# First 512 tokens of a retention layer with its feed-forward block: k and v loaded four tokens to a partition, the work by head pairs on 32-row groups

## The chip, the core and the metric

The kernel runs on one core of one Trainium2 chip. A core has TensorE (PE, matmuls; PEld are its weight loads), VectorE (DVE), ScalarE (ACT), GpSimd (POOL) and SyncE (SP), which here only issues DMAs. Each engine works through its own instruction queue in order and waits on semaphores for the others. The metric is the device time of one execution in microseconds (us).

## The reference

A retention (a recurrent attention with decay) over 4 batches, 8 heads, 768 tokens and head width 64, followed by a feed-forward block over all 3072 tokens.

```python
gamma = 1.0 - 2.0 ** (-5.0 - np.arange(H))
for t in range(S):
    state = gamma[None, :, None, None] * state + np.einsum('bhd,bhe->bhde', k[:, :, t], v[:, :, t])
    y[:, :, t] = scale * np.einsum('bhd,bhde->bhe', q[:, :, t], state)
x = y.transpose(0, 2, 1, 3).reshape(B * S, H * D)
h = x @ w_in                       # 512 -> 2048
g = h * np.tanh(softplus(h))       # Mish
out = g @ w_out                    # 2048 -> 512
```

## The kernel before

Tokens are taken in chunks of C = 128; 24 chunks in all, six to a batch. Retention is done chunkwise: the powers of gamma are folded into q and v when they are cast to 16 bit, k is only scaled. For a chunk, "scores" multiplies k and q (per head, contraction over 64), "mask" keeps the causal part on VectorE (`am`), "present" multiplies v and `am`, "past" multiplies the state and q, and both add up in `y_ps`. "outer" makes k times v, which with the state before and the decay of a chunk (`gcm`) gives the next `state`. Heads are handled in pairs: one head on partitions 0 to 63, the other on 64 to 127, HP = 4 pairs. `xt` takes y for the feed-forward matmuls.

The feed-forward block works on blocks of tokens: first one of 512 tokens (TB; CPB = 4 chunks), then blocks of 256. For the first block `g1` (L412) makes `h_ps`, 16 groups of four matmuls with 512 columns, each followed by a Mish on ScalarE (L420); `g2_mm` (L426) then makes `o_ps`. The matmuls of later blocks carry the retention of the chunks ahead in between, at places that `plan` and `plan_of` write out by hand. The order of instructions on each engine is that of the program (`manual_schedule`); the framework adds the waits.

`first_block` (L570) is the part that has nothing to hide behind. It loads q for all 512 tokens with four neighbouring tokens in one partition (`load_first_q`, L177: runs of 1 KB in memory, two DMAs of 512 KB), k and v chunk by chunk (`load_one`, L120: one token to a partition, runs of 256 B, 256 KB each), and then the weights (`load_weights`, L550: w_in in slices, w_out after it). All these loads are issued by SP, in this order. Since q's tokens stand by residue (token 4p + r), its transpose `qfirst_t` is kept as [pair, r, p], and the scores of chunk g read columns 32g to 32g + 31 of each r; the mask `tri_first` has its columns in the same order, and so has y until `xt_first` (L336) puts it in `xt`. The output of the block is stored in the same order (L434).

The loop at L589 takes the four chunks one after the other: scores, mask (L283), y of the chunk before, outer product with the state before added by an identity matmul (L296), turning k of the next chunk (L206, copied at L208), new state (L303). The last chunk's y is done in two halves. `spin` (L243) and `spin_quarters` (L251) are filler matmuls on the identity, whose results are overwritten. k is scaled on ScalarE (L220), v on POOL (L223). Then `cast_win` (L152) casts w_in on VectorE, half a slice at a time, and the `g1` groups start.

PSUM has two pools: `mmps` (tag "mm", four buffers: t_ps, u_ps, y_ps, h_ps, o_ps) and `atps` (tag "at", two buffers of double size).

## Time and profile before

| what | us |
|---|---|
| runs of the kernel, median of 3 (lowest, highest) | 208.75 (208.70, 208.92) |
| span of the profiled execution, first to last instruction | 206.5 |
| first cast of q starts | 5.26 |
| first chunk's scores (L273) start | 9.84 |
| last cast of v starts | 17.29 |
| last two casts to xt start (L358) | 18.73 |
| h_ps starts (L412) | 19.49 |
| o_ps starts (L426) | 33.55 |

The profile is of one execution; its own device time beside the span isn't recorded, the span is 2.25 us below the median of the runs. In the page, busy times are sums over the span; the chain of waits follows the last instruction back to what released it; the timeline gives start and duration of merged instructions; the windows give busy time per engine in a stretch. The granted clock of TensorE is 0.999 over the span.

### The profile page before, as it was taken

Reading aid. Unit: us, or ns where it says so; the run is one execution under the profiler, and the core shown is the slowest. Engines: PE = TensorE matmul, PEld = TensorE weight load, DVE = VectorE, ACT = ScalarE, POOL = GpSimd, SP = SyncE. Lnnn points to the kernel's source line nnn. Section 1 sums busy time; section 2 is a strip of 40 time slices with the busy share of each in tenths; the row PEclk is TensorE's granted clock in tenths of the full one; section 3 lists DMA queues with packets and bytes.
Section 4 is the critical chain, followed back from the end, with each engine's and each line's share of the span. In section 5 each row is a group of like instructions: output and inputs, shape, how many; then the busy total and the mean of one; then the engine's idle time right before and its main releaser. Section 6 shows DMA issues by size and latency. Waiting matters only on the chain.

```text
span 206.5 us, 4747 instructions
## 1 busy us (share of the span) xinstructions
PE 200.1 (97%) x2005; PEld 151.0 (73%) x2005; DVE 120.7 (58%) x184; ACT 86.5 (42%) x146; POOL 76.2 (37%) x72
## 2 busy tenths in 40 slices
PE   7899999999999999999999999999999999999993
PEld 2465444455855865788888888888888888898882
DVE  2697454267019998475585774495675773572062
ACT  2243664142631541453453453453453453552640
POOL 3242000427866555578665265156266000000000
PEclk9999999999999999999999999999999999999999
DMA  5999999999899999999999798499894800200202
GB/s 175 237 219 345 381 387 355 233 296 208 176 205 292 195 228 207 213 238 253 209 218 152 168 195 149 115 246 154 200 241 71 206 0 2 105 0 27 77 25 76
DMA packets 99988, 38.59 MB, mean 187 GB/s; under 512 B 90496, under 2 KB 94080, under 8 KB 99968
## 3 DMA queue, kind: packets, MB, share of 16 engines
q1 hardware_dynamic: 96704, 37.50, 82.4%
q10 hardware_dynamic: 3264, 0.81, 2.4%
q8 instruction: 15, 0.25, 0.5%
q14 instruction: 5, 0.04, 0.1%
HBM read 27.29 MB, written 6.29 MB: 163 GB/s over the span
## 4 chain that ended last, share of the span: by engine, by line
PE 83%; SPq 7%; DMA 5%; DVE 1%; ACT 1%; issue 1%; ACTq 0%
PE h_ps L412 38%; PE o_ps L506 23%; PE o_ps L426 13%; SPq L122 5%; DMA wi<-in_moe_w_in_dram 5%; PE y_ps L323 3%; PE at L273 3%; PE y_ps L313 2%; SPq L140 2%; PE u_ps L291 2%; ACT xt L400 1%; DVE gsum L476 1%; SPq L181 0%; DVE win L157 0%; PE t_ps L261 0%
## 5 line engine op out<-in xcount | busy, mean ns | idle before, releaser
L412 PE MATMUL h_ps<-xt,win 128*128 128x256 f16 (+1 forms) x704 | 88.0, 282 | 0.4 <-ACT xt L400 0.2
L420 ACT ACTIVATE g<-h_ps 128x512 f16<-128x512 f32 x96 | 57.3, 597 | 57.6 <-PE h_ps L412 57.6
L412 PEld LDWEIGHTS <-win 128*128 128x128 f16 x704 | 67.9, 98 | 16.9 <-DVE win L157 0.9
L217 POOL TENSOR_TENSOR qk<-qf,qvs 128x512 f16<-128x512 f32 x20 | 21.5, 1077 | 61.6 <-DMA qf<-in_q_dram 52.3
L283 DVE TENSOR_TENSOR am<-at,tri 128x1024 f16<-128x1024 f32 x20 | 23.7, 1220 | 17.1 <-PE at L273 16.9
L223 POOL TENSOR_TENSOR v<-vf,qvs 128x512 f16<-128x512 f32 x24 | 25.4, 1059 | 18.6 <-DMA vf<-in_v_dram 17.0
L426 PE MATMUL o_ps<-wout,g 128*128 128x512 f16 x128 | 30.1, 380 | 0.0
L222 POOL TENSOR_SCALAR qk<-kf 128x512 f16<-128x512 f32 x18 | 27.7, 1540 | 2.0 <-DMA kf<-in_k_dram 0.7
L506 PEld LDWEIGHTS <-gsum 128*128 128x128 f16 x256 | 24.4, 98 | 3.8 <-DVE gsum L476 0.4
L506 PE MATMUL o_ps<-tmat,gsum 128*128 128x256 f16 x192 | 23.7, 273 | 0.1
L426 PEld LDWEIGHTS <-g 128*128 128x128 f16 x128 | 11.7, 98 | 13.0 <-issue 0.3
L520 DVE TENSOR_TENSOR osb<-o_ps,snap 128x256 f32<-128x256 f32 x24 | 10.1, 422 | 18.8 <-ACT snap L512 15.7
L506 PEld LDWEIGHTS <-g 128*128 128x128 f16 x192 | 18.8, 98 | 2.2
L400 ACT CAST xt<-y_ps 128x1024 f16<-128x1024 f32 x10 | 10.1, 1012 | 21.7 <-PE y_ps L323 21.7
L475 DVE TENSOR_TENSOR gsum<-g 128x512 f16<-128x512 f16 x16 | 7.6, 472 | 13.6 <-ACT g L420 13.6
L506 PE MATMUL o_ps<-wout,g 128*128 128x256 f16 x128 | 15.3, 273 | 0.0
L512 ACT COPY snap<-o_ps 128x256 f32<-128x256 f32 x24 | 8.9, 372 | 14.0 <-PE o_ps L506 14.0
L306 DVE TENSOR_TENSOR su<-u_ps,st 128x512 f32<-128x512 f32 x13 | 9.0, 691 | 4.7 <-PE u_ps L291 4.5
L307 DVE TENSOR_TENSOR st<-su,gcm 128x512 f16<-128x512 f32 x13 | 9.8, 754 | 0.4
L243 PE MATMUL at<-ident 128*128 128x512 f16 (+1 forms) x26 | 8.0, 440 | 1.3 <-POOL ident L81 1.3
L220 ACT ACTIVATE qk<-kf 128x512 f16<-128x512 f32 x6 | 3.8, 630 | 12.4 <-DMA kf<-in_k_dram 12.4
L157 DVE CAST win<-wi 128x1024 f16<-128x1024 f32 x8 | 5.4, 692 | 5.3 <-DMA wi<-in_moe_w_in_dram 5.3
(61 smaller groups left out, 150.0 us busy)
## 6 DMA issues: line engine op xcount, KB each, us to landing
kf<-in_k_dram SPq DMA_DIRECT2D x23, 256.0 KB, 4.9
vf<-in_v_dram SPq DMA_DIRECT2D x23, 256.0 KB, 5.0
out_dram<-osb SPq DMA_DIRECT2D x22, 256.0 KB, 4.0
qf<-in_q_dram SPq DMA_DIRECT2D x19, 256.0 KB, 4.4
wt<-in_moe_w_out_dram SPq DMA_DIRECT2D x3, 1024.0 KB, 10.1
wi<-in_moe_w_in_dram SPq DMA_DIRECT2D x4, 512.0 KB, 6.9
wi<-in_moe_w_in_dram SPq DMA_DIRECT2D x2, 1024.0 KB, 10.3
qfirst<-in_q_dram SPq DMA_DIRECT2D x2, 512.0 KB, 5.0
```

What stands on the lines that cost most here:

```text
L122: queue.dma_start(loaded[g][n], (q, k, v)[n][b, :, c * C:(c + 1) * C].rearrange("h p d -> p h d"))
L217: nc.gpsimd.tensor_tensor(q16, qf, qs.unsqueeze(2).broadcast_to((P, H, D)), op=ALU.mult)
L222: nc.gpsimd.tensor_scalar(k16, kf, BOOST, None, op0=ALU.mult)
L223: nc.gpsimd.tensor_tensor(v16, vf, vs.unsqueeze(2).broadcast_to((P, H, D)), op=ALU.mult)
L283: nc.vector.tensor_tensor(am[:, :, i:i + n], at[:, :, i:i + n], keep.unsqueeze(1).unsqueeze(1).broadcast_to((P, 2, n, C)), op=ALU.mult)
L307: nc.vector.tensor_tensor(st, su, gcm, op=ALU.mult)
L400: nc.scalar.copy(xt[:, :, :2 * C], y_ps.rearrange("p i j c -> p i (j c)"))
L412: nc.tensor.matmul(h_ps[:, j], wins[s][f // 2][:, bp, f % 2 * P:(f % 2 + 1) * P], xts[blk][:, bp, :nt], start=(bp == 0), stop=(bp == NBP - 1))
L420: nc.scalar.activation(gt, h_ps, AF.Mish, scale=inv_boost3)
L426: nc.tensor.matmul(o_ps, gts[blk, fb][:, t * P:(t + 1) * P], wouts[s][:, f, cols], start=(fb == 0), stop=(fb == NFB - 1))
L506: nc.tensor.matmul(o_ps, x(f), w(f), start=first and f == 0, stop=f == n - 1, skip_group_check=True)
L520: nc.vector.tensor_tensor(dst, o_ps, plus, op=ALU.add)
```

## The change

For the first 512 tokens k and v are loaded like q, four tokens to a partition, and all three by head pairs: twelve DMAs of 256 KB with runs of 1 KB, in the order q0 k0 q1 k1 v0 v1 q2 k2 v2 q3 k3 v3 (`first_loads`). A partition now holds tokens of one chunk in each group of 32 rows (chunk c on rows 32c to 32c + 31). So the work goes by pairs, not by chunks: a pair's scores for all four chunks are 32 matmuls, whose weights are 64 rows by 32 columns (`score_pair`); outer products and "present" take weights of 32 rows by 64 columns; neighbouring matmuls lie on other rows. One mask per pair covers the four chunks; `tri_first` is now made of four selects on POOL and four copies on VectorE. States inside the block are kept as [128, pair, 64] in `early`, and stepped through the chunks by `state_steps`; the state after the fourth chunk goes to the old form. For pair 3 the states are stepped on ScalarE. The first two groups of h_ps are cut into halves: the part over pairs 0 and 1 ahead of the last y, the other part after it (`g1_part`); the half slice of w_in for it is cast on POOL. Of the filler matmuls 28 and 4 (in units of 128 columns) are left. The rest of the program is the same.

```diff
...
-    spread = [qs_np[(jj * CPB + r) % C] for r in range(CPB)]
-    qvs_np = np.ascontiguousarray(np.concatenate([qs_np, vs_np, *spread], 1))
+    spread = [(jj * CPB + r) % C for r in range(CPB)]
+    qvs_np = np.ascontiguousarray(np.concatenate(
+        [qs_np, vs_np] + [qs_np[j] for j in spread] + [vs_np[j] for j in spread], 1))
...
-    tpp = ctx.enter_context(tc.tile_pool(name="rn_tp", bufs=2))
+    tpp = ctx.enter_context(tc.tile_pool(name="rn_tp", bufs=4))
...
+    late = cpool.tile([P, 2 * CPB - 1, Q0], FP32, name="late")
+    tri_first = cpool.tile([P, CPB, CPB, Q0], FP32, name="tri_first")
+    nc.gpsimd.memset(late, 0.0)
+    for c in range(CPB):
+        t = late[c * Q0:(c + 1) * Q0]
+        nc.gpsimd.affine_select(
+            out=t, in_=t, compare_op=ALU.is_gt, fill=1.0, base=CPB - 1,
+            pattern=[[-1, 2 * CPB - 1], [-CPB, Q0]], channel_multiplier=CPB)
...
+    for h in range(H):
+        o = 64 * (h % 2)
+        nc.vector.memset(gc[o:o + 64, h // 2], float(gamma[h] ** C))
+    for r in range(CPB):
+        nc.vector.tensor_copy(tri_first[:, r], late[:, CPB - 1 - r:2 * CPB - 1 - r])
...
-    def cast_win(s):
...
+    def cast_win(s, half, eng):
...
-    def load_first_q():
-    def turn_first_q(qf, half, on_act):
-    def turn_k(g):
-    def spin_quarters(g, n, width):
-    def outer_one(g):
-    def xt_first(g, pairs=slice(None)):
-    def y_one(g):
-    def y_one_in_halves(g):
...
+    def g1_part(h_ps, u, part):
+        for bp in range(2 * part, 2 * part + 2):
+            nc.tensor.matmul(
+                h_ps[:, 0], win(0, u, bp), xts[0][:, bp], start=(bp == 0), stop=(bp == NBP - 1),
+                skip_group_check=True)
...
+    def first_loads():
+        for nm, i in (("q", 0), ("k", 0), ("q", 1), ("k", 1), ("v", 0), ("v", 1),
+                      ("q", 2), ("k", 2), ("v", 2), ("q", 3), ("k", 3), ("v", 3)):
+            t = lpool.tile([P, 2, CPB, D], FP32, name=nm + "f", tag=nm + "f", bufs=4 if nm == "q" else 6)
+            nc.sync.dma_start(
+                t, dict(q=q, k=k, v=v)[nm][0, 2 * i:2 * i + 2, :TB].rearrange(
+                    "h (p r) d -> p h r d", r=CPB))
+            raw[nm, i] = t
+        nload[0] = ncast[0] = CPB
+        load_weights()
...
+    def cast_pair(nm, i, eng):
+        if nm == "q":
+            qk16[i] = castp.tile([P, 2, CPB, 2, D], FP16, name="qk16")
+        if nm == "v":
+            v16p[i] = castp.tile([P, CPB, 2, D], FP16, name="v16")
+        dst = (v16p[i] if nm == "v" else qk16[i][:, "qk".index(nm)]).rearrange(
+            "p r h d -> p h r d")
+        src = raw.pop((nm, i))
+        if nm == "k":
+            nc.scalar.mul(dst, src, BOOST)
+        else:
+            by = (qs_spread if nm == "q" else vs_spread)[:, 2 * i:2 * i + 2]
+            eng.tensor_tensor(
+                dst, src, by.unsqueeze(3).broadcast_to((P, 2, CPB, D)), op=ALU.mult)
+
+    def turn_pair(nm, i, eng):
+        n = "qk".index(nm)
+        if i not in turned:
+            turned[i] = (mmps.tile([P, 2, CPB, P], FP16, name="t_ps", tag="mm"),
+                         qktp.tile([P, 2, CPB, P], FP16, name="qkt", bufs=4))
+        t_ps, qkt = turned[i]
+        for r in range(CPB):
+            nc.tensor.transpose(t_ps[:, n, r], qk16[i][:, n, r], ident)
+        if eng is nc.scalar:
+            nc.scalar.copy(qkt[:, n], t_ps[:, n])
+        else:
+            eng.tensor_copy(qkt[:, n], t_ps[:, n])
+        qkt2[i] = qkt
+
+    def score_pair(i, at):
+        for r in range(CPB):
+            for c in range(CPB):
+                for hh in range(2):
+                    o = slice(64 * hh, 64 * hh + 64)
+                    nc.tensor.matmul(
+                        at[rows(c), hh, r], qkt2[i][o, 1, r, rows(c)],
+                        qkt2[i][o, 0, :, rows(c)], start=True, stop=True,
+                        skip_group_check=True)
+
+    def mask_pair(i, at, hh=slice(0, 2)):
+        if i not in amp:
+            amp[i] = tpp.tile([P, 2, CPB, C], FP16, name="am")
+        nc.vector.tensor_tensor(
+            amp[i][:, hh].rearrange("p a r t -> p a (r t)"),
+            at[:, hh].rearrange("p a r t -> p a (r t)"),
+            tri_first.rearrange("p r a t -> p (r a t)").unsqueeze(1).broadcast_to(
+                (P, hh.stop - hh.start, CPB * C)), op=ALU.mult)
+
+    def state_steps(pairs, on_act=False):
+        n = len(pairs)
+        u_ps = [mmps.tile([P, 2, n, D], FP32, name="u_ps", tag="mm") for _ in range(2)]
+        for c in range(CPB):
+            if c % 2 == 0:
+                for j, i in enumerate(pairs):
+                    for r in range(CPB):
+                        for cc in (c, c + 1):
+                            for hh in range(2):
+                                nc.tensor.matmul(
+                                    u_ps[cc % 2][64 * hh:64 * hh + 64, cc // 2, j],
+                                    qk16[i][rows(cc), 1, r, hh], v16p[i][rows(cc), r, hh],
+                                    start=c == 0 and j == 0 and r == 0, stop=r == CPB - 1,
+                                    skip_group_check=True)
+            u = u_ps[c % 2][:, c // 2]
+            here = slice(pairs[0], pairs[-1] + 1)
+            if c > 0:
+                nc.tensor.matmul(
+                    u, ident, early[c - 1][:, here], start=False, stop=True,
+                    skip_group_check=True)
+            if c == CPB - 1:
+                for hh in range(2):
+                    o = slice(64 * hh, 64 * hh + 64)
+                    nc.vector.tensor_tensor(
+                        states[c][o, here, o], u[o], gc[o, here], op=ALU.mult)
+            elif on_act:
+                for j, i in enumerate(pairs):
+                    nc.scalar.mul(early[c][:, i], u[:, j], gc[:, i, :1])
+            else:
+                nc.vector.tensor_tensor(early[c][:, here], u, gc[:, here], op=ALU.mult)
+            yield
+
+    def y_at(y, off, c, i):
+        j = i % 2
+        return y[:, c % 2, off + j * C:off + (j + 1) * C]
+
+    def y_present(i, y, off, cs, fresh):
+        for r in range(CPB):
+            for c in cs:
+                for hh in range(2):
+                    nc.tensor.matmul(
+                        y_at(y, off, c, i)[64 * hh:64 * hh + 64], v16p[i][rows(c), r, hh],
+                        amp[i][rows(c), hh, r], start=fresh and r == 0,
+                        stop=c == 0 and r == CPB - 1, skip_group_check=True)
+
+    def y_past(i, y, off, cs):
+        for c in cs:
+            for hh in range(2):
+                o = slice(64 * hh, 64 * hh + 64)
+                nc.tensor.matmul(
+                    y_at(y, off, c, i)[o], early[c - 1][o, i], qkt2[i][o, 0, :, rows(c)],
+                    start=False, stop=True, skip_group_check=True)
+
+    def y_out(half, y, off, cs, eng):
+        dst = xts[0][:, 2 * half:2 * half + 2].rearrange(
+            "p i (r c t) -> p c (i r) t", r=CPB, c=CPB)[:, cs[0]:cs[1] + 1]
+        src = y[:, :, off:off + 2 * C].rearrange("p c (a t) -> p c a t", t=Q0)
+        if eng is nc.scalar:
+            nc.scalar.copy(dst, src)
+        else:
+            eng.tensor_copy(dst, src)
...
+    def first_retention():
+        xts[0] = xtp.tile([P, HP, TB], FP16, name="xt")
+        states[CPB - 1] = stp.tile([P, HP, P], FP16, name="st")
+        nc.gpsimd.memset(states[CPB - 1], 0.0)
+        for c in range(CPB - 1):
+            early[c] = stp.tile([P, HP, D], FP16, name=f"early{c}", bufs=1)
+        at = at_tile()
+        spin(at, 28)
+        cast_pair("q", 0, nc.vector)
+        cast_pair("k", 0, nc.scalar)
+        turn_pair("q", 0, nc.vector)
+        turn_pair("k", 0, nc.scalar)
+        cast_pair("q", 1, nc.vector)
+        cast_pair("k", 1, nc.scalar)
+        cast_pair("v", 0, nc.gpsimd)
+        cast_pair("v", 1, nc.gpsimd)
+        turn_pair("q", 1, nc.vector)
+        score_pair(0, at)
+        mask_pair(0, at)
+        turn_pair("k", 1, nc.scalar)
+        at = at_tile()
+        spin(at, 4)
+        score_pair(1, at)
+        mask_pair(1, at)
+        cast_pair("q", 2, nc.gpsimd)
+        cast_pair("k", 2, nc.scalar)
+        steps = state_steps((0, 1))
+        next(steps)
+        turn_pair("k", 2, nc.scalar)
+        cast_pair("v", 2, nc.gpsimd)
+        cast_pair("q", 3, nc.gpsimd)
+        cast_pair("v", 3, nc.gpsimd)
+        at = at_tile()
+        next(steps)
+        y = y_tile()
+        for i in range(2):
+            y_present(i, y, 0, (0, 1), i == 0)
+        for i in range(2):
+            y_past(i, y, 0, (1,))
+        y_out(0, y, 0, (0, 1), nc.scalar)
+        turn_pair("q", 2, nc.vector)
+        next(steps)
+        cast_pair("k", 3, nc.scalar)
+        score_pair(2, at)
+        mask_pair(2, at)
+        next(steps)
+        for i in range(2):
+            y_present(i, y, 2 * C, (2, 3), False)
+        for i in range(2):
+            y_past(i, y, 2 * C, (2, 3))
+        turn_pair("k", 3, nc.scalar)
+        y_out(0, y, 2 * C, (2, 3), nc.scalar)
+        steps = state_steps((2,))
+        next(steps)
+        turn_pair("q", 3, nc.scalar)
+        next(steps)
+        at = at_tile()
+        score_pair(3, at)
+        mask_pair(3, at, slice(0, 1))
+        last = state_steps((3,), True)
+        next(last)
+        next(steps)
+        mask_pair(3, at, slice(1, 2))
+        next(last)
+        ya = y_tile()
+        y_present(2, ya, 0, (0, 1), True)
+        y_past(2, ya, 0, (1,))
+        next(steps)
+        next(last)
+        cast_win(0, 0, nc.gpsimd)
+        h_ps = [mmps.tile([P, 1, TB], FP32, name="h_ps", tag="mm") for _ in range(2)]
+        for u in range(2):
+            g1_part(h_ps[u], u, 0)
+        y_present(3, ya, 0, (0, 1), False)
+        y_past(3, ya, 0, (1,))
+        y_out(1, ya, 0, (0, 1), nc.scalar)
+        yb = y_tile()
+        for i in (2, 3):
+            y_present(i, yb, 0, (2, 3), i == 2)
+        for i in (2, 3):
+            y_past(i, yb, 0, (2, 3))
+        y_out(1, yb, 0, (2, 3), nc.vector)
+        next(last)
+        return h_ps
     def first_block():
...
+        first_loads()
+        h_ps = first_retention()
+        for u in range(2):
+            g1_part(h_ps[u], u, 1)
+            mish(0, u, h_ps[u])
+        cast_win(0, 1, nc.vector)
         for s in range(1, NSL):
-            cast_win(s)
+            for half in range(2):
+                cast_win(s, half, nc.vector)
...
-        for u in range(2 * NFB):
+        for u in range(2, 2 * NFB):
```

187 lines of the change are left out of this document (48 added, 139 removed).

## The prediction

> **What bounds the kernel now.** I read the page's busy shares first, then the chain of waits in order of time, then the timeline and the two-microsecond windows of the first 20 us.
>
> ```profile
> span 206.5 us, 4747 instructions
> PE 200.1 (97%) x2005; PEld 151.0 (73%) x2005; DVE 120.7 (58%) x184; ACT 86.5 (42%) x146; POOL 76.2 (37%) x72
> ```
>
> PE is full: whatever starts the stream of h_ps matmuls (L412) later or earlier moves the end by as much. The chain says what starts it.
>
> ```profile
> 10.00 1.11 SPq L122
> ...
> 16.44 9.41 DMA wi<-in_moe_w_in_dram
> 25.88 0.70 DVE win L157
> 26.63 7.08 PE h_ps L412 x32
> 33.71 0.65 PE o_ps L426 x3
> ```
>
> Up to 26.6 us it is loads only (SP issuing k and v, then w_in), afterwards PE to the end. No retention step is in it. The windows (columns: window, length, busy us of PE, PEld, DVE, ACT, POOL, then clock, DMA share, GB/s) tell how far behind the retention is:
>
> ```profile
> 4.00:6.00 2.00, 2.00 (x9) 0.69 (x7) 0.74 (x1) 0.00 (x0) 0.00 (x0) 1.00 1.12 356
> ...
> 12.00:14.00 2.00, 1.96 (x51) 1.28 (x55) 1.75 (x3) 1.10 (x2) 0.66 (x1) 1.00 1.39 228
> 14.00:16.00 2.00, 1.92 (x67) 1.38 (x53) 2.00 (x3) 0.87 (x2) 1.04 (x1) 1.00 1.15 243
> ```
>
> q, in 1 KB runs, flows at 356 GB/s; k and v, in 256 B runs, at about 230. But at that pace VectorE is already nearly full: a chunk costs it 0.42 (L208) + 0.68 (L303) + 1.22 (L283) = 2.32 us, and chunks come every 2.4. Faster loads have little to release unless VectorE's work changes.
>
> ```profile
> 1.34 4.76 PE L243 MATMUL at<-ident 128*128 128x512 f16 x14 [1.34 <-POOL ident L81]
> ...
> 5.26 1.23 DVE L189 TENSOR_TENSOR qfirst<-qfirst,qvs 128x1024 f16<-128x1024 f32 x1 [2.53 <-DMA qfirst<-in_q_dram]
> ...
> 11.37 0.47 PEld L251 LDWEIGHTS <-ident 64*64 64x64 f16 x48
> ...
> 12.42 1.22 DVE L283 TENSOR_TENSOR am<-at,tri_first 128x1024 f16<-128x1024 f32 x1
> ...
> 14.38 0.40 PE L273 MATMUL at<-qfirst_t,kt 64*128 64x128 f16 x8
> ...
> 16.25 0.26 PEld L251 LDWEIGHTS <-ident 64*64 64x64 f16 x16
> ...
> 17.29 1.04 POOL L223 TENSOR_TENSOR v<-vf,qvs 128x512 f16<-128x512 f32 x1 [2.23 <-DMA vf<-in_v_dram]
> ...
> 18.74 0.69 DVE L157 CAST win<-wi 128x1024 f16<-128x1024 f32 x1 [0.16 <-DMA wi<-in_moe_w_in_dram]
> ...
> 19.49 14.22 PE L412 MATMUL h_ps<-xt,win 128*128 128x512 f16 x64
> ```
>
> The mark to beat: h_ps starts at 19.49 and its 64 matmuls hand over to o_ps at 33.55 (0.22 us each).
>
> **The loads.** The two 512 KB halves of q were used at 5.26 and 6.76, so 1 KB runs bring 256 KB in 0.74 us. All twelve new loads have such runs: q0 lands at 4.5, k0 5.3, q1 6.0, k1 6.7, then one each 0.74, the last v at 12.6 instead of 17.29; the first half slice of w_in, 1.45 behind it as now (17.29 to 18.74), at 14.1. SP issues the same bytes in 12 loads instead of 10; at 0.5 us an issue (L181, 0.96 for two) that stays ahead. The third slice of w_in, the one that holds PE now at 26.6, comes at 21.2. Loads leave the path.
>
> **The preamble.** VectorE gets eight more 64x64 memsets (1.25 us, the time of the eight L99 ones) and four copies of 128x128 (0.15 each, like one of those memsets) that wait for POOL's new mask: a memset and four selects of 224 columns. A select of 128 columns and its gap to the next instruction took 0.24 here, at most 0.54 by scaling the 0.31 one to 224; I take 0.42. POOL is done at 1.3 + 0.3 + 1.7 = 3.3; VectorE then copies (0.6) and does the old gcm memsets (0.48 + 1.25): the first cast of q starts at 5.6, 1.1 after its data. Bounds 5.1 to 6.1.
>
> **The small matmuls.** Scores, outer products and y become 128 each of 64x32 or 32x64 tiles (the old ones: 32, 16 and 32). No such tile is in the trace. The nearest rows are the quarter tiles of L251: 48 of 64 columns in 0.47 us of weight loads (10 ns each), 16 of 128 columns in 0.26 (16 ns). Four tiles at once thus turn over in 40 and 64 ns. I take 10 ns for the outer products and 16 for y (four tiles side by side in each) and 10 for scores (eight tiles; the least seen). The upper bound is the half tiles: eight L273 in 0.33, 41 ns. Each change of tile shape costs too: four full L313 take 0.32 (14.71 to 15.03) where four of 55 ns are 0.22, so about 0.08; the new order has some thirty such changes.
>
> The page "TensorE: Matmul & The Clock Gate" of the Trainium skill, in its section "Wait — 56ns, not 53.3ns?", puts the least start-to-start time at about 25 ns however small a matmul is. The 48 in 0.47 contradict it; by the rule the walk below would grow by about 3.9 us, to some 215.
>
> **VectorE's work.** Two casts of q at 0.65 (half of 1.23), three copies of turned q at 0.42, masks 3 x 1.22 + 2 x 0.68, state steps that shrink from 0.68 to 0.28 and 0.21 but become three times as many (3.0 together, counting the writes to the last state), one copy of xt 0.68: about 11.2 us against 12.5 before. From 5.6 that alone reaches 16.8, if it never waits. The new order then has the first half of two h_ps groups behind it, four matmuls, which the old one has at 19.49 + 0.88 = 20.4: no more than 3.6 us of gain is possible (205.1).
>
> **The walk.** It does wait, since the chunks' states now follow each other through VectorE and PE in steps of about 0.5 us, in line with masks and copies. I follow the four queues in program order, each step at the later of its engine's last end and its inputs plus 0.05 (L208 ends 9.78, L273 starts 9.83), 0.17 from a matmul's last issue to its end. Pair 0: cast 5.6 to 6.2, turned, copied by 7.1; k shares q's PSUM tile, so its transposes wait for that copy; ScalarE's copy (0.57, as L349) ends 8.2, scores 8.8, mask 10.06. Pair 1: k's cast queues on ScalarE behind that copy, scores 10.4, mask 11.66. The first state step is queued behind this mask: 11.84; y of pairs 0 and 1, first half, 12.97; the turn of q2 is behind it on PE, its copy 13.75, scores 2 at 14.3, mask 2 at 15.6, the last state of pairs 0 and 1 at 15.97. Pair 2's outer products need the PSUM buffer which that frees: 16.3. q3's turn is behind them, its copy on ScalarE behind k3's copy and the xt copy: 17.46. Scores 3 at 18.0, its two masks at 18.8 and 19.5, states to 20.0, y of pairs 2 and 3 to 22.17, xt copy on VectorE 22.22 to 22.90. Only then the second half of the first two h_ps. The six casts on POOL (1.04 each) and its w_in half (about 2, from 14.1) end ahead of their users; the other w_in casts (0.69) stand behind the xt copy and feed two groups of four matmuls (1.76) each: hidden.
>
> **Sum.** At 22.95 two half groups and fourteen whole ones are left: 60 matmuls x 0.22 = 13.2, so o_ps at 36.1 against 33.55: 2.55 later. After that PE idles little (9.96 of 10 us busy from 40 to 50) and nothing of it changes. The first w_out load waits for both casts of the first w_in slice, now done at 23.8 instead of 20.9; with the 10.1 us to landing of the page and a cast of 1.23 (L167) it is ready at 35.2, just ahead of 36.1, the next ones have 3.5 us more each. The profiled span, 206.5, lies 2.25 below the median of the runs, 208.75; I take what lies around it as unchanged: 208.75 + 2.55 = **211.3 us**. Own range: 209.2 (no cost of tile changes, preamble at its lower bound, -1.6, hand-offs 0.03) to 213.7 (16 ns scores and outer products +1.1, shape changes 0.11 +0.6, preamble +0.5).
>
> **Rivals.** *Slow array* (0.15; 212.3 to 215.7). The first nine L243 come at 0.43 us, the later ones at 0.2: the array speeds up only after 3.4 us without a pause. Before, 54 + 14 + 8 + 8 columns-of-128 of filler and small ones later keep it going; now seven matmuls end near 4.4 and PE pauses until 6.2, then mostly waits. Slow until 13 us it costs 1.0; slow into the h_ps stream 1.7 there (eight at 0.43) and some 2.7 ahead: 4.4. Against it: the reading of the granted clock is 1.00 even while they take 0.43, so the page can't tell. The same page of the Trainium skill, in its part 1 on the clock gate, says a pause under about 3.4 us does not slow a warm array but that it warms only after a busy window of that length; by it this rival hangs on whether three microseconds are enough.
>
> *Small matmuls at the pace of half tiles* (0.08): 25 to 41 ns each, 215 to 221.
>
> *The runs of 1 KB bring nothing for k and v* (0.04): 1.2 us a load as now, last v at 17.9, PE waits for pair 3: 213.7.
>
> *The loads were all that mattered* (0.16; faster, about 206.7). For it: the chain names only loads. If the retention followed the last v as closely as now (17.29 to 19.49), h_ps would start at 14.8. Against it: VectorE's sum above, which stops it at 205.1. It decides once the way from first cast to second half of h_ps is below 14.7 us instead of my 17.3, that is with hand-offs and shape changes nearly free.
>
> *A draw* (0.07), gains and losses meeting within 0.2%, about what a measurement here can tell.
>
> **Numbers.** My forecast has 0.50. Slower: 0.50 + 0.15 + 0.08 + 0.04 = 0.77; same 0.07; faster 0.16. The range 207.7 to 214.9 leaves out about 0.1 on each side.
>
> **What would show it.** The last v cast near 12.7 (loads); VectorE's first cast at 5.6; each 32 scores within 0.4; xt's last copy at 22.2; the first 16 whole h_ps at 0.22 and not 0.43; wins waited for by nobody. The forecast is wrong if that xt copy ends before 20.3, or if h_ps after it runs slow.

## The result and the profile after

The changed kernel takes 221.92 us (median of 4 runs, 221.79 to 222.80) against 208.73 of the kernel before, run beside it: ratio 1.063 [1.060, 1.066]. The forecast was 211.3 us, with a range of 207.7 to 214.9. The direction was right, the size was not: 10.6 us are missing. The profiled execution has a span of 221.0 us against 206.5. Here and below a time is the median of all executions, a ratio with its 95% interval compares undisturbed ones alone, and the traces of e5, e6, e13 and e16 are of disturbed, slower executions.

First the page: busy time of TensorE, and the DMA queue that brings instructions (packets, MB, share); behind it the line of that queue before.

```profile
span 221.0 us, 5182 instructions
...
PE 206.9 (94%) x2205; PEld 154.9 (70%) x2205; DVE 122.3 (55%) x202; ACT 88.3 (40%) x151; POOL 83.2 (38%) x79
...
q8 instruction: 17, 0.28, 0.6%
```

```profile
q8 instruction: 15, 0.25, 0.5%
```

PE has 200 more matmuls, so 400 more instructions (a matmul is a weight load and a matmul). The instruction queue moved 0.28 MB in 17 packets, 16 KB each; 17 times 256 is 4352, about the two times 2205 instructions of PE. So a packet is a block of 256 instructions (64 bytes each). Before, 15 packets and 2005 matmuls fit the same way (15 times 256 is 3840, of 4010). The line was on the page before, and the prediction passed over it.

The chain of waits (start, us, what) now has retention in it all the way to the second half of h_ps at 30.84, and two things that were not there:

```profile
16.64 1.09 issue
...
30.84 1.89 PE h_ps L365 x4
32.73 12.95 PE h_ps L358 x56
45.70 8.50 DMA kf<-in_k_dram
```

"issue" is time in which PE waited for nothing that the profile shows. o_ps starts at 45.50 (before: 33.55), and behind it a load of k for a later chunk is on the chain.

The timeline (start, us, engine, line, operation, tiles, count, idle before and its releaser):

```profile
6.01 0.69 DVE L541 TENSOR_TENSOR qk<-qf,qvs 128x512 f16<-128x512 f32 x1
...
9.14 0.36 PEld L563 LDWEIGHTS <-qkt 64*32 64x32 f16 x32 [0.32 <-ACT qkt L553]
...
13.37 1.05 POOL L541 TENSOR_TENSOR v<-vf,qvs 128x512 f16<-128x512 f32 x1
14.60 1.04 POOL L169 CAST win<-wi 128x1024 f16<-128x1024 f32 x1 [0.17 <-DMA wi<-in_moe_w_in_dram]
...
16.03 0.61 PE L563 MATMUL at<-qkt 64*32 64x128 f16 x25
17.73 0.31 PE L563 MATMUL at<-qkt 64*32 64x128 f16 x7 [1.09 <-issue]
...
22.85 0.43 PE L586 MATMUL u_ps<-v,qk 32*64 32x64 f16 x23
23.93 0.32 PE L586 MATMUL u_ps<-v,qk 32*64 32x64 f16 x9 [0.65 <-issue]
...
28.41 1.07 PE L617 MATMUL y_ps<-am,v 32*64 32x128 f16 x32
...
30.09 0.69 DVE L637 CAST xt<-y_ps 128x512 f16<-128x512 f32 x1 [4.15 <-PE y_ps L626]
...
30.84 1.89 PE L365 MATMUL h_ps<-xt,win 128*128 128x512 f16 x4 [0.62 <-DVE xt L637]
```

Four things are to be read here. The loads came as forecast: the last v is cast at 13.37 and then only because POOL has a cast of q ahead of it, the first half slice of w_in at 14.60 (before: 17.29 and 18.74). The four h_ps matmuls take 1.89, 0.43 between starts, twice the 0.22 of before: the array is at half pace. Twice PE stops in the middle of 32 matmuls of one kind whose inputs are all there, after the 25th and the 23rd. And the last copy to xt ends at 30.78, forecast 22.90.

The pace has to be read from durations. The granted clock of this execution reads 1.00 throughout. The trace's own record of clock changes holds, for this kernel, no entry before 34.32 us: full speed from there. For the kernel before it holds full speed from 4.77 us.

Two windows (window, length, busy us of PE, PEld, DVE, ACT, POOL, then clock, DMA share, GB/s), the second of them as it was before, and the line of SP's waits for w_out (total, times, longest):

```profile
26.00:28.00 2.00, 2.00 (x20) 0.70 (x18) 0.00 (x0) 0.31 (x1) 0.00 (x0) 1.00 0.00 0
...
50.00:55.00 5.00, 3.08 (x19) 1.48 (x18) 0.00 (x0) 0.77 (x2) 0.00 (x0) 1.00 1.32 227
```

```profile
50.00:55.00 5.00, 4.86 (x44) 3.83 (x40) 1.29 (x2) 2.93 (x5) 4.84 (x4) 1.00 0.87 182
```

```profile
SPq L154 <- DVE win L169: 19.1, 3, 17.1
```

From 24 to 32 us the DMA engines have next to nothing to do, since the loads of w_out need the buffers of w_in, whose casts stand on VectorE behind the copy to xt. Between 50 and 55 PE then idles 1.9 of 5 us (0.14 before): it waits for the cast of k of a later chunk, whose load has come late.

The sum of the difference: o_ps 11.95 later and 1.8 us more of idle time at 50 to 55, together 13.7 of the 14.5 us between the spans.

### The profile page after: what moved, and what is told of

Read it like the earlier page. It is cut to its first block, busy times and chain, and to the rows that moved or that the text cites. A ratio compares the mean times of both kernels' runs of the same rounds, so it can differ in the third digit from the quotient of the medians.

```text
span 221.0 us, 5182 instructions
## 1 busy us (share of the span) xinstructions
PE 206.9 (94%) x2205; PEld 154.9 (70%) x2205; DVE 122.3 (55%) x202; ACT 88.3 (40%) x151; POOL 83.2 (38%) x79
## 4 chain that ended last, share of the span: by engine, by line
PE 83%; DVE 6%; DMA 4%; ACT 3%; issue 2%; POOL 1%; POOLq 0%; ACTq 0%; DVEq 0%
PE h_ps L358 38%; PE o_ps L451 20%; PE o_ps L371 8%; DMA kf<-in_k_dram 4%; PE y_ps L284 3%; PE at L241 3%; PE y_ps L617 2%; PE y_ps L274 2%; PE h_ps L365 2%; PE u_ps L255 2%; PE t_ps L551 2%; PE at L563 1%; DVE gsum L421 1%; ACT qkt L553 1%; ACT xt L331 1%
## 5 line engine op out<-in xcount | busy, mean ns | idle before, releaser
L358 PE MATMUL h_ps<-xt,win 128*128 128x256 f16 (+1 forms) x696 | 87.0, 283 | 0.3 <-ACT xt L331 0.2
L194 POOL TENSOR_TENSOR qk<-qf,qvs 128x512 f16<-128x512 f32 x20 | 22.0, 1101 | 82.3 <-DMA qf<-in_q_dram 79.4
L199 POOL TENSOR_SCALAR qk<-kf 128x512 f16<-128x512 f32 x18 | 28.2, 1564 | 2.3 <-DMA kf<-in_k_dram 1.1
L200 POOL TENSOR_TENSOR v<-vf,qvs 128x512 f16<-128x512 f32 x20 | 22.1, 1103 | 2.2 <-PE o_ps L371 0.8
L420 DVE TENSOR_TENSOR gsum<-g 128x512 f16<-128x512 f16 x16 | 8.6, 538 | 13.2 <-ACT g L347 13.2
L421 DVE TENSOR_TENSOR gsum<-gsum,g 128x512 f16<-128x512 f16 x16 | 8.8, 551 | 0.5
L451 PE MATMUL o_ps<-tmat,g 128*128 128x256 f16 x64 | 8.3, 273 | 0.0
L451 PE MATMUL o_ps<-wout,gsum 128*128 128x256 f16 x64 | 8.3, 273 | 0.0
```

Of the source, the lines that this page charges most:

```text
L194: nc.gpsimd.tensor_tensor(q16, qf, qs.unsqueeze(2).broadcast_to((P, H, D)), op=ALU.mult)
L199: nc.gpsimd.tensor_scalar(k16, kf, BOOST, None, op0=ALU.mult)
L200: nc.gpsimd.tensor_tensor(v16, vf, vs.unsqueeze(2).broadcast_to((P, H, D)), op=ALU.mult)
L358: nc.tensor.matmul(h_ps[:, j], win(s, f, bp), xts[blk][:, bp, :nt], start=(bp == 0), stop=(bp == NBP - 1))
L421: nc.vector.tensor_tensor(s2, s1, a11, op=ALU.subtract)
L451: nc.tensor.matmul(o_ps, x(f), w(f), start=first and f == 0, stop=f == n - 1, skip_group_check=True)
```

## The experiments

The first theory was the rival of the forecast, the slow array. The second: PE's instructions arrive in blocks of 256, and the block isn't there when PE needs it. Counted in the order of the program, the two pauses lie exactly 256 instructions apart, at 448 and 704. The third: the late w_out. The table gathers the runs on the changed kernel; "h_ps" is the start of the second half of the first h_ps (forecast 22.95), "full pace" is from the trace's record of clock changes, "pauses" are those that the timeline puts down to issue (the 1.2 of e9 is explained below).

| run | us | ratio to before | h_ps | full pace, us | pauses, us |
|---|---|---|---|---|---|
| after | 221.92 | 1.063 [1.060, 1.066] | 30.84 | from 34.32 | 1.09, 0.65 |
| e1a_filler_start | 221.16 | 1.060 [1.058, 1.062] | 30.44 | 5.50 to 12.32, from 36.22 | 1.54, 0.55 |
| e1b_filler_all | 219.25 | 1.052 [1.049, 1.055] | 29.20 | 6.07 to 16.31, from 23.14 | 2.29 |
| e4_more_instructions | 223.15 | one run | 31.58 | from 36.41 | 1.69, 0.51 |
| e7_w_in_held | 219.99 | 1.054 [1.050, 1.058] | 29.41 | no entry, slow at h_ps | 0.61 |
| e11_lean_filler | 221.92 | 1.061 [1.057, 1.065] | 31.00 | 7.14 to 17.38, from 34.44 | 2.22, 0.30 |
| e9_lean_filler_held | 216.74 | 1.038 [1.031, 1.045] | 26.61 | 6.15 to 26.63, from 30.05 | 1.52, 1.2 |
| e2_casts_first | 220.81 | 1.058 [1.055, 1.062] | 31.35 | from 37.20 | 1.11, 0.92 |
| e8_three_together | 221.50 | 1.062 [1.057, 1.066] | 31.42 | 6.37 to 26.85, from 37.09 | 2.47 |
| e10_lean_held_casts | 216.49 | 1.037 [1.033, 1.041] | 26.77 | 4.20 to 21.26, from 31.50 | 0.96 |
| e13_lean_held_longer | 218.19 | not settled | 26.00 | 6.52 to 20.17, from 30.41 but for 50.89 to 54.30 | none |
| e16_held_longer_filler_back | 214.76 | 1.022 [1.019, 1.025] | 25.23 | 4.97 to 22.03, from 28.86 | none |
| e17_held_longer_more_filler | 218.54 | 1.051 [1.044, 1.059] | 27.48 | 4.34 to 24.82, from 31.65 | 3.04 |

### Is it the array's pace? (e1a_filler_start, e1b_filler_all, e5_before_no_filler)

Filler as long as before at the start; then filler at eight more places that wait.

```diff
-        spin(at, 28)
+        spin(at, 54)
```

> The changed kernel with 54 instead of 28 units of filler at the start, as the kernel before has; nothing else. Theory (the array runs at half pace until it has been busy for 3.4 us without a pause, and the change never gives it that before h_ps): transposes after the first cast come at 55 ns instead of 107, the first h_ps at 0.22 instead of 0.43, the last xt copy moves from 30.1 to about 25.5, and the time falls by 6 to 7 us, to about 215. Rival 1 (low use of the array slows it again, however it was started): warm for the first few us only, 0.5 to 1.5 us saved, h_ps still at 0.43 at first. Rival 2 (hand-offs and instruction supply, not pace): less than 1 us.

```diff
-        spin(at, 28)
+        spin(at, 54)
...
+        spin(at, 12)
...
+        spin(at, 8)
...
-        spin(at, 4)
+        spin(at, 12)
...
+        spin(at, 16)
...
+        spin(at, 8)
...
+        spin(at, 12)
...
+        spin(at, 12)
...
+        spin(ya.rearrange("p a (m c) -> p a m c", c=C), 8)
```

> The changed kernel with 54 units of filler at the start and 8 to 16 more ahead of eight waits of TensorE on the way. Theory (pace of the array): at least what the filler at the start alone gives, h_ps at 0.22 from its first matmul, 214 to 216 us. If the array slows again at low use, this one is faster than the one with filler at the start alone by several us; if not, it is equal to it or slower by the filler's own time on the path, up to 1 us.

The start alone brought 0.76 us, with intervals that overlap, and not the 6 to 7 of the theory; the first rival had it right. The array was at full pace from 5.50, but at 12.32 it fell back. The timeline of PE in e1a, the longest idle in the 3.4 us before that, and h_ps:

```profile
12.32 0.27 PE L594 MATMUL u_ps<-early,ident 128*128 128x128 f16 x1 [0.88 <-DVE early L606]
...
30.44 1.89 PE L365 MATMUL h_ps<-xt,win 128*128 128x512 f16 x4 [0.62 <-DVE xt L637]
```

So no pause of 3.4 us is needed: a stretch whose longest pauses were 0.88 and 0.46 was enough. Beside this rival the prediction had set a rule of the Trainium skill (page "TensorE: Matmul & The Clock Gate", part 1), by which a pause under about 3.4 us leaves a warm array alone; this run shows otherwise. The full stretches in the record are 6.83, 10.24, 13.65, 17.07 and 20.48 us, multiples of 3.41, which agrees with the length of the window that this page of the Trainium skill gives.

With filler everywhere it was faster by 2.7 us, less than half of what was expected, and the pace came back in time for h_ps (1.04 for four), but a pause in the scores of pair 2 is now 2.29 us, and the array fell back in it. The same places of e1b:

```profile
17.22 0.61 PE L563 MATMUL at<-qkt 64*32 64x128 f16 x27 [2.29 <-issue]
...
29.20 1.04 PE L365 MATMUL h_ps<-xt,win 128*128 128x512 f16 x4 [0.65 <-DVE xt L637]
```

The cross-check takes filler out of the kernel before: only its first one is left, at 28.

```diff
-        spin(0, 54)
+        spin(0, 28)
...
-        spin(0, 14)
...
-                spin(g + 1, 2 if g else 8)
...
-                spin_quarters(g + 1, (48, 40, 16)[g], C // 2 if g < 2 else C)
```

> The kernel before with 28 units of filler at the start, as in the changed kernel, and no other. Theory (pace of the array): the first h_ps run at 0.43 us, the retention takes longer, and the time grows by 2 to 6 us, to 211 to 215, although nothing but useless matmuls is gone. Rival (filler does nothing here because loads set the pace until 26.6 us): within 0.5 us of 208.7.

214.10 us, 1.022 [1.015, 1.029]: leaving useless matmuls out makes the old kernel slower, by the ratio 4.6 us. A window and the timeline of its profiled execution:

```profile
8.00:12.00 4.00, 2.65 (x27) 1.93 (x24) 2.53 (x5) 0.94 (x2) 1.84 (x2) 0.50 1.37 218
```

```profile
22.41 15.02 PE L412 MATMUL h_ps<-xt,win 128*128 128x512 f16 x64
```

The clock column reads 0.50 here, because in this execution the record has entries from 4.02 on (half pace from 7.43 to 24.50); h_ps starts 2.92 later than before and takes 0.8 longer. The pace of the array is a real part of it, but not the whole.

### Do instructions come late? (e4_more_instructions, e7_w_in_held, e11_lean_filler, e9_lean_filler_held)

If the pauses hang on a count, more instructions ahead of them must move them forward. The first filler, 7 matmuls of 512 columns, becomes 28 of 128: the same work, 42 instructions more.

```diff
-        spin(at, 28)
+        for _ in range(28):
+            spin(at, 1)
```

> The changed kernel with its first filler cut into 28 matmuls of 128 columns instead of seven of 512: 42 instructions more on TensorE (with their weight loads) and the same columns. Theory (TensorE waits for its next 256 instructions to be fetched when small matmuls use them up fast): the pause of 1.09 us that now comes after the 25th of pair 2's 32 score matmuls comes 42 instructions earlier, after about the fourth, and that of 0.65 us after the 23rd outer product also 42 earlier. Rival (the pause belongs to these matmuls or to their data): both stay where they are. The time is the same within 1 us.

42 instructions are 21 matmuls; the pause moved from behind the 25th of the 32 scores to behind the 4th, and the second one from behind the 23rd outer product to behind the 2nd (0.51 us before 24.21). Timeline of PE:

```profile
16.03 0.29 PE L563 MATMUL at<-qkt 64*32 64x128 f16 x4
18.01 0.61 PE L563 MATMUL at<-qkt 64*32 64x128 f16 x28 [1.69 <-issue]
```

It ends when the block arrives. In the trace's list of DMA packets the transfer of 16 KB starts at 15.42 there (15.09 in after), takes 1.16 us, and the first instruction behind it starts 1.4 us after it is complete. Why so late? The loads of w_in fill the DMA engines at that time (351 to 392 GB/s from 14 to 22 us). So the next run holds the loads of w_in back until the last cast of v, by a write of one element into the buffer behind that cast on POOL.

```diff
         if which == "in":
             t = wstage.tile([P, NBP, TB], FP32, name="wi", tag="wt", bufs=4)
+            if s == 0:
+                nc.gpsimd.memset(t[:, 0, :1], 0.0)
...
-        load_weights()
...
         cast_pair("v", 3, nc.gpsimd)
+        load_weights()
```

> The changed kernel with the w_in loads held back until POOL has cast the last v (about 14.4 us; a one-element memset on the tile makes them wait). Theory (the fetch of TensorE's next 256 instructions queues behind the loads): the first fetch, now from 15.1 to 16.3, starts near 13 in the stretch without loads, and the pause of 1.09 us after the 25th score matmul of pair 2 disappears; w_in still lands before it is used; 220.5 to 221.2 us. Rival (the fetch takes as long whatever the loads do): the pause stays, the time is 221.8 or more, since w_in comes 6 us later.

The block's transfer starts at 12.06 instead of 15.09 and the first pause is gone, though PE executes the same instructions up to it. Timeline of PE in e7:

```profile
16.02 0.63 PE L564 MATMUL at<-qkt 64*32 64x128 f16 x32
```

In both runs PE starts instruction 192, the edge of the block before, at 11.6. The next transfer follows 3.5 us later in after and 0.4 in e7: it had not been fetched ahead, and its delay is what the loads change. The time fell by 1.9 us; the second pause stays, and so does the slow array. The pair that isolates the supply is filler at full pace ("lean": few, large filler matmuls), without and with the hold:

```diff
-        spin(at, 28)
+        spin(at, 54)
...
+        spin(at, 8)
...
+        spin(at, 4)
...
-        spin(at, 4)
+        spin(at, 8)
...
+        spin(at, 8)
...
+        spin(at, 4)
...
+        spin(at, 8)
...
+        spin(at, 8)
```

> The changed kernel with the same lean filler but w_in not held back. Theory (instruction supply starts the trouble: the pause near 15 to 17 us lets the array fall back): a pause of 1.5 to 2.5 us in pair 2's scores, slow from about 16 to 20 us or longer, last xt copy 3 us or more behind that of the kernel with w_in held back, 215 to 219 us. Rival (filler alone keeps the pace): within 1 us of the kernel with w_in held back.

> The changed kernel with w_in held back and with less filler than before throughout (18 matmuls of 512 columns more than in the change instead of 23), so that the third block of 256 instructions is first needed behind the last y. Theory (slow array and instruction supply are what the forecast lacked): no pause of TensorE longer than 0.3 us without a visible wait before h_ps, the array at full pace from 6 us on, last xt copy at 22.5 to 24 us, h_ps at 0.22, 211.5 to 214 us; w_out still late. Rival (the supply of instructions is not what made the pauses): pauses at other places, above 217.

221.92 without, 216.74 with: 5.2 us from nothing but the time at which w_in is loaded. Both lie above what was expected of them. Up to the first edge the two run alike (instruction 447 starts at 14.74 and 14.39); there e11 pauses. Timeline of e11, then that of e9:

```profile
17.21 0.40 PE L563 MATMUL at<-qkt 64*32 64x128 f16 x21 [2.22 <-issue]
```

```profile
8.81 0.24 PEld L564 LDWEIGHTS <-qkt 64*32 64x32 f16 x32 [0.26 <-ACT qkt L554]
...
18.65 0.24 PE L587 MATMUL u_ps<-v,qk 32*64 32x64 f16 x5
20.42 0.36 PE L587 MATMUL u_ps<-v,qk 32*64 32x64 f16 x27 [1.52 <-issue]
...
26.61 1.87 PE L367 MATMUL h_ps<-xt,win 128*128 128x512 f16 x4 [1.87 <-DVE win L171]
```

At full pace the 32 scores take 0.24 of weight loads (0.36 in after): 7.5 ns each, where the prediction had 10. The pause at instruction 704 is left, now 1.52 (transfer at 18.11, under the load of w_in), and one at 960, just ahead of h_ps. The profile names a cast of w_in as the releaser there, but that first half slice had been used at 22.15; the transfer of the block runs from 24.16 to 25.29 and PE goes on 1.3 later, as at the other pauses. Of the 1.87 us the first part is the copy to xt: the weight load of the same matmul, the last instruction ahead of the edge, starts right behind it at 25.40. That leaves 1.2 for the block.

### The same on the kernel before (e12_before_more_instr)

```diff
-        spin(0, 54)
+        for _ in range(54):
+            spin(0, 1)
```

> The kernel before with its first filler cut into 54 matmuls of 128 columns instead of 14 of at most 512: 80 instructions more on TensorE, the same columns, nothing else. Theory (256 instructions at a time, about 6 us apart while loads run, and the kernel before just keeps within it): a pause of about 1 us near 15 to 16 us, ahead of the last chunk's scores, and 1 to 4 us more in all, the upper end if the array then falls back: 209.7 to 212.7. Rival (no limit there): within 0.4 us of 208.6.

210.10 us, 1.007 [1.005, 1.010], with no pause for instructions at all. The mechanism that was expected did not show; the time rose for another reason. The blocks were fetched earlier (12.33 and 18.03 instead of 13.87 and 20.71), amid the loads of k and v, and the third v came late. POOL and PE in its timeline:

```profile
15.13 1.04 POOL L223 TENSOR_TENSOR v<-vf,qvs 128x512 f16<-128x512 f32 x1 [2.48 <-DMA vf<-in_v_dram]
...
16.22 0.38 PE L291 MATMUL u_ps<-v,qk 128*128 128x128 f16 x4 [0.73 <-POOL v L223]
```

That cast started at 14.02 before. That the block's transfer pushed the load back is argued from the times, not shown.

### The late w_out (e2_casts_first)

All casts of w_in on VectorE go ahead of the last copy to xt.

```diff
         next(last)
+        cast_win(0, 1, nc.vector)
+        for s in range(1, NSL):
+            for half in range(2):
+                cast_win(s, half, nc.vector)
```

> The changed kernel with the w_in casts on VectorE moved ahead of the last xt copy; nothing else. Theory (w_out, and behind it k and q of the fifth chunk, are issued only when w_in is cast, and the casts stand behind the late xt copy, so that DMA is idle from 24 to 32 us and TensorE waits 1.9 us between 50 and 60): the first w_out load is issued near 27 instead of 32, that wait goes, 219.5 to 220.3 us. Rival (the wait has another cause, such as the order of the plan): unchanged within 0.3 us, 221.8.

The loads of w_out are issued at 27.03 instead of 32.06, and PE is busy for 5.00 of the 5 us from 50 to 55: the wait of 1.9 is gone. But the time fell only by 1.1, less than expected and with intervals that overlap, since h_ps starts 0.5 later behind the casts and the array stays slow until 37.2. This wait is a part of the loss.

### Putting the remedies together (e8, e10, e13, e16, e17)

The first attempt joined all of e1b, e2 and e7.

> The changed kernel with filler throughout, w_in casts ahead of the last xt copy, and w_in held back, together. Theory (slow array, instruction supply and late w_out make up what the forecast lacked): the array stays at full pace from 6 us on, no pause for instructions, the last xt copy at 23 to 25 us, 211 to 213.5 us, which is the forecast of the change. If it stays above 215, something else is missing in the walk. Rival: the three overlap, 217 to 218.

It came out at 221.50. The last y was done at 26.3 in spite of a pause of 2.47 at instruction 960, but the copy to xt then stood until 30.68 behind casts of a w_in that had been held back. That is a fault of the combination and says nothing on the causes. With lean filler and only two of the casts moved:

> The one before this with two of the w_in casts ahead of the last xt copy. Theory (w_out is issued late since w_in is cast late): w_out some 1.5 us earlier, 0 to 1 us less than without it, 211 to 213.5 us. Rival (w_in, held back, lands too late for these casts, and the xt copy waits behind them): 1 to 2 us more.

216.49, no better than e9 within the intervals, though nothing waits at 50 to 55 any more. Then w_in was held longer, until VectorE had masked pair 2, with two filler matmuls fewer (the lines of the hold, against e9):

```diff
-                nc.gpsimd.memset(t[:, 0, :1], 0.0)
+                nc.vector.memset(t[:, 0, :1], 0.0)
...
         mask_pair(2, at)
+        load_weights()
```

> The lean filler version with w_in held back, but held until VectorE has masked pair 2 (about 16) instead of until the last v cast (about 14), and with two of the filler matmuls of 512 columns left out. If what is left between 216.7 us and the forecast of 211.3 us is the two pauses in which TensorE has no instructions (1.52 and 1.87 us in the lean, held version) and the slow array that follows the second: the block of instructions at row 704 is fetched before the loads of w_in are dense, that pause goes, and the time is 213 to 215.5 us; if the second pause goes too and the array stays at full pace, 211.5 to 213. If the rest has another cause (late w_in, say), the time stays at 216 to 218; a w_in that is now late itself would show as a wait of TensorE for a cast of w_in at 22 to 27.

No pause for instructions was left, as expected, but the array fell back at 20.17, and four executions spread from 214.56 to 219.28. With the two filler matmuls (0.43 us of work) put back, and with four more:

> The version with w_in held until the mask of pair 2, with the two filler matmuls of 512 columns put back that the last run left out. In that run no pause for instructions was left, but the array fell to half pace at 20.17, after a stretch with too little use, and stayed there for 10.24 us. If those two matmuls are what the stretch lacked: no pause for instructions, full pace until h_ps, the second half of the first h_ps before 25, and 212.5 to 215 us. If the hold itself is what costs (w_in late, casts late): 217 to 219 as before, with waits of TensorE for casts of w_in.

> The same with four more filler matmuls of 512 columns (two in each of the two places around the scores of pair 3). If use of the array in that stretch decides: full pace to h_ps at least as surely as in the run beside it, and 212.5 to 215 us; up to 0.8 us more than that one where it is already at full pace, because the filler then lies on the path. If the filler is not what decides: 217 to 219.

214.76 and 218.54. The timeline of e16, then that of e17:

```profile
18.00 0.42 PE L564 MATMUL at<-qkt 64*32 64x128 f16 x32
...
21.00 1.04 PE L367 MATMUL h_ps<-xt,win 128*128 128x512 f16 x4 [0.71 <-POOL win L171]
...
22.76 1.07 PE L618 MATMUL y_ps<-am,v 32*64 32x128 f16 x32
```

```profile
22.36 0.64 PE L618 MATMUL y_ps<-am,v 32*64 32x128 f16 x32
...
26.32 0.37 PE L627 MATMUL y_ps<-qkt,early 64*64 64x128 f16 x3 [3.04 <-issue]
```

e17 has four filler matmuls, 0.86 us of work, more than e16. In these traces they keep the array at full pace through y (0.64, in e16 1.07), and their eight instructions bring the edge of the next block ahead of the last y, where PE then waits 3.04 us. In e16 the same edge lies behind it. The expectation for e17 was wrong in its number, 3 us too low: it had reckoned with pace alone. e16 is the best of the changed kernels. Its trace is of an execution of 216.54 us, 5.2 above the forecast, and shows 3.4 of these: y at half pace 0.93 (21.97 to 24.44, 1.54 in e9), the 3.6 us of h_ps at half pace 1.8, the wait for a held-back w_in 0.71. Two of its four executions took 212.68 and 213.21, which lies within the forecast's range.

### What are the loads in 1 KB runs worth? (e6_before_1k_runs, e14_1k_runs_few_fillers, e15_before_few_fillers)

The kernel before with k and v loaded in 1 KB runs; its retention then works on the wrong order of k and v, so the first 512 tokens come out differently.

```diff
-            load_one(g, 1, nc.sync)
-            load_one(g, 2, nc.sync)
+            for n in (1, 2):
+                nc.sync.dma_start(
+                    loaded[g][n].rearrange("p (h r) d -> p h r d", r=CPB),
+                    (q, k, v)[n][0, 2 * g:2 * g + 2, :TB].rearrange("h (p r) d -> p h r d", r=CPB))
```

> The kernel before with k and v of the first 512 tokens loaded in runs of 1 KB, as the change loads them, and all else as it was; the retention of these tokens then works on the wrong order of k and v, so the output of the first block is another. What the loads alone are worth. Forecast's view (VectorE needs 2.32 us a chunk and is nearly full already): last v cast near 13 to 17 instead of 17.3, h_ps starts 0.5 to 2 us earlier, 206.8 to 208.3 us. Rival (loads are all that counts): h_ps starts near 15 to 16, 204.5 to 205.5 us. Rival 2 (w_in and w_out set the start anyway): no change.

211.80 us, 1.013 [1.009, 1.016]: slower, where no theory had it so. The timeline says why:

```profile
17.49 0.32 PE L273 MATMUL at<-qfirst_t,kt 64*128 64x128 f16 x5 [1.17 <-issue]
```

The last v is cast at 12.3, so PE reaches instruction 448 earlier, while the block's transfer starts later (14.87 instead of 13.87): w_in is now loading at the full rate. PE pauses, and the array falls back from 18.82 to 22.24. In the kernel before the block was just in time. To test this, the 104 quarter-array fillers were replaced by 5 matmuls of 512 columns, some 200 instructions fewer, with the 1 KB loads and, as the control, with the old ones:

```diff
-                spin_quarters(g + 1, (48, 40, 16)[g], C // 2 if g < 2 else C)
+                spin(g + 1, (8, 8, 4)[g])
```

> The kernel before with k and v loaded in 1 KB runs (its retention then works on the wrong order of k and v) and with its 104 quarter-array filler matmuls replaced by 5 of 512 columns, about 198 instructions fewer. If the 1 KB runs cost time in the earlier run (1.013 of before) only because the instructions of TensorE came too late: no pause for instructions before h_ps, h_ps starts at 18 to 19 and the time is 206.5 to 208.3 us. If loads in 1 KB runs are no gain in any case: 208.7 or more.

> The kernel before with its 104 quarter-array filler matmuls replaced by 5 of 512 columns. Control for the run with 1 KB loads: if the supply of instructions does not hold the kernel before, 208.4 to 209.2 us, the same as before within 0.3 us. If the quarter-array filler did more than keep the array in use, or the fewer instructions free the loads, the time moves by more than 0.5 us.

With 1 KB loads 207.88 us, 0.996 [0.994, 0.998]; the control 209.23, 1.003 [1.002, 1.005]. POOL and PE of the first:

```profile
12.31 1.04 POOL L223 TENSOR_TENSOR v<-vf,qvs 128x512 f16<-128x512 f32 x1 [0.48 <-DMA vf<-in_v_dram]
...
18.52 3.83 PE L412 MATMUL h_ps<-xt,win 128*128 128x512 f16 x17
```

No pause for instructions, and h_ps starts at 18.52 (control 19.97). So the loads are worth 1.35 us as soon as the supply keeps up, and cost 2.7 (by the ratio of e6) when it doesn't. This version is no replacement for the kernel before, since its output differs; no version with the right output was faster than it.

## Why the prediction was right or wrong

**What bounds the kernel.** That whatever starts the stream of h_ps matmuls "later or earlier moves the end by as much" held: o_ps 11.95 later, 14.5 in the span. That the retention would now set that start, and that this makes it slower, held too: e16, with most of the lost pace and supply given back, is still at 1.022.

**The loads.** That "1 KB runs bring 256 KB in 0.74 us" held in its effect: first half slice of w_in used at 14.60, forecast 14.1. "Loads leave the path" failed in a way that the step hadn't looked for: w_in now flows at the full rate from 14 us on, and the instructions of PE come late when such loads run. The rival that 1 KB brings nothing is refuted by the control pair (1.35 us).

**The preamble.** First cast of q at 5.6, bounds 5.1 to 6.1; measured 6.01.

**The small matmuls.** 10, 10 and 16 ns for scores, outer products and y. At full pace e9 has 0.24 for 32 scores (7.5 ns), 0.33 for 32 outer products (10), 0.48 for 32 of y (15). The rates were right, and the 25 ns of the page "TensorE: Matmul & The Clock Gate" of the Trainium skill do not hold for such tiles, which lie side by side in the array. In after the same groups took 0.36, 0.51 and 0.82, since the array ran at half pace. What the step left out is that each of these matmuls is two instructions, at a rate at which the supply doesn't follow: at 10 ns the 128 matmuls of a block are through in 1.3 us, while its transfer alone takes 1.1 and the first instruction comes 1.2 to 1.5 after it. Two of the prediction's sums are slightly off: the cost of a change of shape is 0.32 - 0.22 = 0.10 and not 0.08, and the upper end of the own range adds up to 213.5 and not 213.7.

**The walk.** This is the step that failed. Copy of xt from 22.22, measured 30.09. Its order and hand-offs were right as far as they can be followed: in e16, with pace and supply in place up to 22, the scores of pair 2 start at 14.35 and end at 14.77 (forecast end 14.3) and those of pair 3 start at 18.00 (forecast end 18.0), although filler lies between them. Two assumptions failed under it: that every matmul runs at full pace (in after none does before 34.32), and that PE always has its next instruction, a term that the walk put at nothing without a reason (1.09 and 0.65 us of pauses in after, up to 3.04 in other versions).

**The sum.** "60 matmuls x 0.22" was wrong for those before 34.32, which took 0.43. That w_out is "ready at 35.2, just ahead of 36.1" was wrong: the sum took the casts of w_in as done by 23.8, yet they stand behind the copy to xt, which was 7.9 late. That behind o_ps "nothing of it changes" then cost 1.8 us; e2 shows the link. In the profiled execution this makes 7.9 for the second half of h_ps (30.84 for 22.95), 1.5 for its 60 matmuls (14.7 for 13.2) and 1.8 for the wait: 11.2 of the 11.95 us by which its span exceeds the forecast one.

**The rivals.** The slow array, held at 0.15, was what happened, and for longer than its price (212.3 to 215.7) allowed, all through the retention. The prediction had the evidence: the first nine matmuls at 0.43 under a reading of 1.00, the missing filler. All it held against it was that the granted clock can't tell, and the rule of the Trainium skill on the length of pauses, which it set beside that, did not hold in e1a. "The loads were all that mattered" is refuted by e6 and e14 together, in which the loads alone move the time by +2.7 or -1.35 us. The supply of instructions was in no rival.

So of the 10.6 us beyond the forecast most are one lost condition, a TensorE at full pace with its next instruction at hand, with two causes that feed each other: fewer fillers and more, smaller instructions. The late w_out is the rest. Filler alone in its lean form brings nothing (e11), the hold alone 1.9 (e7), both 5.2 (e9), a longer hold 7.2 by the medians and 8.6 by the ratios (e16). What share each would have by itself can't be stated, since a pause for instructions also slows the array.

## What to carry to other kernels

Count instructions as a resource: where a stage turns matmuls into many small ones, work out where every 256th instruction of TensorE falls and what the DMA engines do at that time; a bulk load that starts a few microseconds earlier can starve the engine. Filler that looks useless holds the pace of the array, but where the supply is short it should be few large matmuls, not many small ones (e14 against e6); where it isn't, that brought nothing (e15, 1.003). And judge the pace by the time of a known matmul (0.22 or 0.43 here), not by the granted clock of a stretch near the start.

## What the runs showed of the hardware that was not expected

- TensorE's instructions arrive in transfers of 16 KB, 256 instructions, by a queue that the page lists with those of the data. A transfer takes 1.0 to 1.2 us in most runs, and where PE waits for it the first instruction starts 1.2 to 1.5 us after its end. In the retention it starts only after PE has come to the edge before (0.4 to 4.9 us after), and under dense loads later still (15.09 against 12.06 for the same block in after and e7). The page "Runtime: NRT & Kernel Launch" of the Trainium skill, section "Instruction fetch mechanics", gives the 16 KiB and 256 instructions, which these runs confirm, and calls the crossing of a boundary mostly hidden, which they don't: pauses of 0.30 to 3.04 us.
- The array falls back to half pace without any long pause: at 12.32 in e1a after idle stretches of 0.88 us at most, at 20.17 in e13 after none above 0.43 in the 3.4 us before. What measure of use decides is open; a pause of 1.52 in e9 did not trigger it.
- A retention of small matmuls needs filler to stay fast, and yet 0.86 us more filler made the kernel 3.8 us slower by the medians, 6 by the ratios (e16, e17); in the traces its eight instructions bring the edge of a block ahead of the end of the last y, where PE waits 3.04 us.
